# Relu rows of the later bias units one step ahead of their products, and the unpacking of the third weight matrix begun at the end of the second stage

## The chip, the cores and the metric

The kernel runs on one core of a Trainium2 chip. The metric is the device time of one execution in microseconds (us); the program is launched once and timed several times.

## What is computed

Attention with a learned position bias, followed by a gated product of matrices. For 4 batches, 8 heads, 576 positions and 64 channels a head:

```python
scores = (q @ k.T) / sqrt(64)
x = log1p(|i - j|) / log1p(max(i, 1))            # one number per pair of positions
bias = relu(x[..., None] * w1 + b1) @ w2         # 32 hidden units, one column of w2 per head
attn = softmax(scores + bias)
y = (attn @ v) as 2304 tokens x 512
out = ((y @ w_a) * (y @ w_b)) @ w_out            # 512 -> 1536 -> 512
```

All in 32-bit floats; the kernel splits operands into two 16-bit (or reduced 32-bit) parts and adds the products.

## The kernel before

**Score tiles.** The scores are made in 144 tiles of up to 128 rows by 576 columns (list `TILES`). The generator `attn_steps` has two steps for each tile. For tile n it loads the bias rows of tile n+2 from DRAM on SP's queue (`load_bias`, line 439), runs the *score step* (`soft1`: line 487 on VectorE adds scores and bias and takes the row minimum, line 492 on ScalarE takes the exponential), makes the score products of the next tile (`qk`, line 459, one PSUM buffer), transposes an earlier tile (`turn`, lines 535, 552, 554) and, once per unit of tiles, multiplies by v (`pv`, line 574). Three buffers hold loaded bias rows, so the load for a new tile waits for the score step three tiles before. `prep_k`, `prep_q` and `prep_v` (lines 385 to 423) prepare operands some tiles ahead.

**The gated products.** `moe_main` multiplies finished tokens by the first two matrices (`ab`, line 666, 24 steps), gates them (lines 674 and 676) and multiplies by the third (`o`, line 715, 12 steps). They fill TensorE between the score products. TensorE's order is the order in which the program is written; the function `merge` deals out the steps of several generators in proportion. The other engines' order is chosen by a scheduler, held by `late()`, which puts an instruction behind the newest score step, exponential and normalisation traced so far on its engine.

**Unpacking the weights.** The matrices arrive as 64-bit words. `w_unit` turns one chunk of 128 x 512 into 32-bit floats: line 256 on ScalarE scales the high words into a tile t, line 258 on VectorE shifts, line 259 merges the low words, line 262 merges the sign. `wo_split` then makes the two parts of a chunk of the third matrix on ScalarE (303) and GpSimd (304). `wo_steps` (its object is called `won`) does the 12 chunks of the third matrix, after a first step that only issues two loads. Raw words have three buffers, the tiles `wt` four.

**The bias table.** It is made on the chip, in 36 units of 16 rows (`bias_unit`). A unit takes the scaled logarithms u, forms four relu rows (line 134 on VectorE, line 138 on ScalarE; `nact` says how many are ScalarE's), multiplies them with w2 (line 144, four short products into PSUM), scales twice into `bo` (lines 161 and 164) and stores that to DRAM (line 166). Units 0 to 15 run at the start; the 20 *later units*, 16 to 35, run as a stream between the score tiles 46 to 61, while the batch that needs them is still to come. `stream[1]` lists at which tile a step of the stream is taken; each step does one unit whole. Their four row buffers h0 to h3 are single. A unit of up to 512 columns takes one of three PSUM buffers, a longer one two. The later units' u is loaded anew (line 117) when the unpacking of the third matrix is through, and scaled at line 119.

**Order around the change.** The second stage (main products of batch 0 beside score tiles 20 to 35) ends with `merge((main, 2 * FC - 19), (asteps, n1 - n1 * 4 // 5))`. The third opens with `merge((main, 2 * FC), (asteps, n2 * 2 // 3), (won, FC + 1))`: 24 product steps, 21 half tiles, and all of the third matrix. Then u is loaded and the stream begins.

Of the kernel before, what the change touches and what calls it, by code (L numbers as in the profile page):

```python
# [7 lines left out]
F32 = mybir.dt.float32  # L8
# [3 lines left out]
I32 = mybir.dt.int32  # L12
# [9 lines left out]
NU = S // 16  # L22
# [25 lines left out]
def attention_moe(ctx, tc, q0d, q1d, kd, vd, idn, wp, wa, wb, wo, lsw, lg, rl, out):  # L48
# [65 lines left out]

    def bias_windows(pool, tag, after=None):
        u = pool.tile([128, S], F32, tag=tag, name="u", bufs=1)
        nc.sync.dma_start(out=u, in_=lsw)
        with tc.issue_after(after.ins) if after else nullcontext():
            nc.vector.tensor_scalar(out=u, in0=u, scalar1=tab["w1"], scalar2=None, op0=ALU.mult)
        return u  # L120

# [23 lines left out]

    def bias_unit(bg, banks, u, un, nact, rows, bufs, queue):
        n = bias_span(un)
        hs = bias_relu(rows, u, un, nact)
        ob = bg.tile([128, BW], F32, tag="bo", name="bo", bufs=bufs)
# [16 lines left out]
        queue.dma_start(out=dst[:, :, :BW - 1], in_=ob[:, :BW - 1])  # L166
        yield

# [12 lines left out]
    @contextmanager  # L181
    def late():
        with ExitStack() as s:
            for x in (ttrs, exps, evs, pns):
                if x:
                    s.enter_context(tc.issue_after(x[-1].ins))
            yield
# [154 lines left out]
    def wo_steps(wt):  # L342
        raws = [w_load(wt, wo, f) for f in range(2)]
        yield
        for f in range(FC):
            with late():
                wf = w_unit(wt, raws[f])
                wo_split(f, wf)
            raws[f] = None
            if f + 2 < FC:  # L350
                raws.append(w_load(wt, wo, f + 2))
            yield
# [425 lines left out]
    with tc.tile_pool(name="bg", bufs=1, side="right") as bg, tc.tile_pool(name="eq", bufs=1, space=PSUM) as eq, \  # L778
# [6 lines left out]
        nc.vector.memset(tab["one"], 1.0)  # L785
        uls = bias_windows(att, "rk")

        def first_units(banks):
            for un in range(NU0):
                hs = cpool[0].tile([128, 4, S], F32, tag="pt", name="h", bufs=2)  # L790
                yield from bias_unit(
                    bh, lambda: banks(un), uls, un, int(un % 2 == 0 or un >= 8), lambda g: hs[:, g], 4, nc.gpsimd
                )

# [33 lines left out]
    run(wab)  # L828
    merge((main, 2 * FC - 19), (asteps, n1 - n1 * 4 // 5))
    ws.close()  # L830
    gpool[0] = ctx.enter_context(tc.tile_pool(name="gp", bufs=1, side="right", reuse_waits="tile"))

    def bias_stream(bg, u):
        for un in range(NU0, NU):
            yield from bias_unit(
                bg, lambda: mps.tile([128, 1, 2 * TOK], F32, tag="ab", name="psta", bufs=3), u, un, int(un % 4 != 3),
                lambda g: bg.tile([128, S], F32, tag=f"h{g}", name=f"h{g}", bufs=1), 2, nc.scalar,
            )

    nb = NU - NU0  # L840
    n2, n3 = steps(2)[1], 2 * ((ends[3] - ends[2]) * 2 // 3)
    main = moe_main(1, 0, mps)
    merge((main, 2 * FC), (asteps, n2 * 2 // 3), (won, FC + 1))
    run(won)
    wstack.close()
    with tc.tile_pool(name="bg2", bufs=1, reuse_waits="tile") as bg:
        uls = bias_windows(bg, "u", last[-12])
        stream[0] = bias_stream(bg, uls)
        first, nst = ends[1] + n2 // 3, ends[2] + n3 // 2 - ends[1] - n2 // 3
        stream[1] = [first + nst * i // nb for i in range(nb)]  # L850
        merge((main, GS + 1), (asteps, n2 - n2 * 2 // 3))
        xpool[0] = ctx.enter_context(tc.tile_pool(name="xp", bufs=1, side="right", reuse_waits="tile"))
        main = moe_main(2, 0, mps)
        merge((main, 2 * FC), (asteps, n3))
        run(stream[0])
# [61 lines left out]
```

## Time and profile before

| | |
|---|---|
| median of three timed runs | 846.47 us (843.23 to 848.3) |
| the profiled execution | 849.39 us, span of its instructions 847.6 us |
| TensorE busy | 775.6 us, 92% of the span |
| VectorE busy | 538.0 us, 63% |
| ScalarE busy | 511.6 us, 60% |
| GpSimd busy | 322.2 us, 38% |
| TensorE's mean granted clock | 0.953 of full speed |

Times in the trace count from the first instruction. PE is TensorE's products, PEld its weight loads, DVE VectorE, ACT ScalarE, POOL GpSimd, SP the engine that issues most loads. "busy" is the time inside instructions; an idle time in square brackets stands ahead of the instruction that ended it, with what released it behind the arrow. The granted clock is the share of full speed that TensorE got in a stretch. The third matrix is unpacked between about 210 and 278 us, the later bias units run from 280 to 382 us.

### The profile page before, as it was taken

Reading aid. Unit: us, or ns where it says so; the run is one execution under the profiler, and the core shown is the slowest. Engines: PE = TensorE matmul, PEld = TensorE weight load, DVE = VectorE, ACT = ScalarE, POOL = GpSimd, SP = SyncE. Lnnn points to the kernel's source line nnn. Section 1 sums busy time; section 2 is a strip of 40 time slices with the busy share of each in tenths; the row PEclk is TensorE's granted clock in tenths of the full one; section 3 lists DMA queues with packets and bytes.
Section 4 is the critical chain, followed back from the end, with each engine's and each line's share of the span. In section 5 each row is a group of like instructions: output and inputs, shape, how many; then the busy total and the mean of one; then the engine's idle time right before and its main releaser. Section 6 shows DMA issues by size and latency. Waiting matters only on the chain.

```text
span 847.6 us, 16500 instructions
## 1 busy us (share of the span) xinstructions
PE 775.6 (92%) x5960; PEld 621.3 (73%) x5960; DVE 538.0 (63%) x1243; ACT 511.6 (60%) x1102; POOL 322.2 (38%) x508
## 2 busy tenths in 40 slices
PE   4786779999878799979999999999999999999998
PEld 1244557668766566658888888988888898888886
DVE  4757778766899467874787777767776774110100
ACT  6667787656877467764676667656665665331310
POOL 1326667552765212321344334433442344220210
PEclk9957788999999799999999999999999999999999
DMA  8888675446773364543445444444434421100001
GB/s 284 282 270 225 204 204 157 138 120 199 225 224 99 98 181 143 152 134 89 140 126 142 137 141 121 113 137 143 122 117 129 129 74 52 58 1 26 2 11 39
DMA packets 51573, 114.16 MB, mean 135 GB/s; under 512 B 5156, under 2 KB 9508, under 8 KB 51492
## 3 DMA queue, kind: packets, MB, share of 16 engines
q1 hardware_dynamic: 44336, 97.34, 39.2%
q10 hardware_dynamic: 5876, 10.93, 4.4%
q0 software_dynamic: 1280, 4.84, 1.6%
q8 instruction: 47, 0.77, 0.4%
q14 instruction: 34, 0.28, 0.1%
HBM read 95.91 MB, written 17.18 MB: 133 GB/s over the span
## 4 chain that ended last, share of the span: by engine, by line
PE 68%; DVE 12%; DMA 9%; ACT 4%; issue 4%; POOL 1%; SPq 1%; ACTq 0%; DVEq 0%; POOLq 0%
PE ab L666 26%; PE o L715 18%; PE tp L535 8%; PE qk L459 8%; PE pv L574 5%; DMA rv<-vd 3%; DVE p L487 3%; PE psta L144 2%; DVE wt L262 2%; DMA bias<-bias_d 1%; DVE ks L386 1%; ACT p L492 1%; DMA rqf<-q0d 1%; DMA wraw<-wa 1%; DMA bias_d<-bo 1%
## 5 line engine op out<-in xcount | busy, mean ns | idle before, releaser
L666 PEld LDWEIGHTS <-w16t 128*128 128x128 f16 x2592 | 252.8, 99 | 46.8 <-issue 16.4
L666 PE MATMUL ab<-x,w16t 128*128 128x256 f16 x2304 | 273.2, 275 | 4.4 <-ACT bo L164 2.5
L487 DVE CUSTOM_DVE_ANT_0 p<-qk,bias 128x576 f32<-128x576 f32 x144 | 108.7, 755 | 92.6 <-PE tp L535 79.7
L522 POOL TENSOR_SCALAR p<-p,sm 128x576 f32<-128x576 f32 x144 | 127.9, 888 | 75.1 <-DVE sm L520 68.3
L552 ACT CAST pt<-tp 128x640 f16<-128x640 f32 x128 | 88.3, 690 | 95.3 <-PE tp L535 94.9
L492 ACT ACTIVATE p<-p,mn 128x576 f32<-128x576 f32 x144 | 111.7, 776 | 42.5 <-DVE mn L487 38.2
L535 PE MATMUL tp<-idn,p 128*128 128x128 f32 x720 | 110.5, 287 | 17.4 <-DVE pt L554 6.6
L715 PE MATMUL o<-wos,gh 128*128 128x512 f32 x384 | 124.4, 405 | 0.0
L691 POOL TENSOR_TENSOR gl<-g,gh 128x256 fp32r<-128x256 f32 x96 | 72.4, 754 | 131.7 <-ACT gh L690 130.5
L519 POOL TENSOR_SCALAR sm<-sm 128x1 f32<-128x1 f32 x144 | 30.2, 210 | 222.0 <-ACT p L492 218.4
L535 PEld LDWEIGHTS tp<-idn,p 128*128 128x128 f32 x720 | 86.7, 146 | 35.8 <-issue 19.9
L676 DVE SCALAR_TENSOR_TENSOR g<-ab,wv,asb 128x256 f32<-128x256 f32 x84 | 40.5, 482 | 81.3 <-ACT asb L674 80.7
L715 PEld LDWEIGHTS o<-wos,gh 128*128 128x128 f32 x384 | 69.1, 190 | 17.8 <-issue 5.4
L459 PE MATMUL qk<-ks,qs 128*128 128x288 f32 x384 | 72.4, 311 | 4.5 <-DVE mn L487 4.4
L715 PE MATMUL o<-wos,gl 128*128 128x512 f32 x192 | 75.7, 394 | 0.0
L144 PE MATMUL psta<-h,w2s 128*32 128x288 f32 (+17 forms) x352 | 50.8, 567 | 25.0 <-DVE h L134 16.4
L459 PEld LDWEIGHTS qk<-ks,qs 128*128 128x128 f32 x384 | 56.8, 190 | 9.7 <-DVE mn L487 6.5
L674 ACT ACTIVATE asb<-ab,wv 128x256 f32<-128x256 f32 x84 | 39.3, 467 | 37.7 <-PE ab L666 37.5
L690 ACT CAST gh<-g 128x256 fp32r<-128x256 f32 x96 | 38.8, 404 | 36.3 <-DVE g L676 36.2
L556 DVE TENSOR_TENSOR pt<-tp,pt 128x512 f16<-128x512 f32 x80 | 55.1, 689 | 8.0 <-ACT pt L552 7.9
L574 PE MATMUL pv<-pt,vs 128*64 128x320 f16 (+1 forms) x808 | 58.3, 299 | 0.0
L134 DVE TENSOR_SCALAR h<-u,lgs 128x576 f32<-128x576 f32 (+17 forms) x117 | 48.4, 471 | 12.6 <-PE psta L144 6.1
(98 smaller groups left out, 1017.6 us busy)
## 6 DMA issues: line engine op xcount, KB each, us to landing
bias<-bias_d SPq DMA_DIRECT2D x128, 288.0 KB
rv<-vd SPq DMA_DIRECT2D x40, 320.0 KB
rk<-kd SPq DMA_DIRECT2D x24, 288.0 KB
wraw<-wa SPq DMA_DIRECT2D x12, 512.0 KB
wraw<-wb SPq DMA_DIRECT2D x12, 512.0 KB
wraw<-wo SPq DMA_DIRECT2D x12, 512.0 KB
bias_d<-bo ACTq DMA_DIRECT2D x20, 295.5 KB
rq<-q1d SPq DMA_DIRECT2D x16, 320.0 KB
```

Of the source, the lines that this page charges most:

```text
L144: nc.tensor.matmul(dst[32 * g:32 * g + 32], tab["w2"], hs[g][:, c0:c1], start=True, stop=True)
L459: nc.tensor.matmul(ps[:, hf, :HB], a, b[:, hf * HB:hf * HB + HB], start=(x == 0), stop=(x == len(prods) - 1))
L487: ttr = nc.vector.tensor_tensor_reduce(out=p.rearrange("p (a n) -> p a n", a=2), in0=ps[:, :, :HB], in1=bt.rearrange("p (a n) -> p a n", a=2),
L492: exps.append(nc.scalar.activation(p, p, AF.Exp, bias=mn, scale=-1.0, accum_out=sm))
L522: nc.gpsimd.tensor_scalar(out=p, in0=p, scalar1=rc, scalar2=1.0, op0=ALU.mult, op1=ALU.mult)
L535: nc.tensor.transpose(tp[:, x, :], p[:, c0:c0 + 128], tab["idn"])
L552: nc.scalar.copy(dst[:, 0:5], src)
L556: nc.vector.tensor_tensor(out=dst[:, 5:9], in0=src[:, 0:4], in1=dst[:, 0:4], op=ALU.subtract)
L574: nc.tensor.matmul(ps[64 * j:64 * j + 64, :N], vs[:, part, vb, j, :], pt[:, pb, j * N:j * N + N], start=(x == 0), stop=(x == len(terms) - 1),)
L666: nc.tensor.matmul(ab[:, j], w16[nm, f][:, pw, kk, :], xs[px][:, kk, :], start=(x % (3 * KC) == 0), stop=(x % (3 * KC) == 3 * KC - 1),)
L691: nc.gpsimd.tensor_tensor(out=gl, in0=g, in1=gh.bitcast(F32), op=ALU.subtract)
L715: nc.tensor.matmul(o, g[:, sl], wos[f][:, p], start=(f == 0 and x == 0), stop=(f == FC - 1 and x == 2))
```

## The change

The relu rows leave `bias_unit`. `bias_stream` now scales u and makes the rows of unit 16 in a first step of its own; each later step makes the products of one unit and behind them the rows of the next, into the same single buffers. The stream so has 21 steps, dealt out over tiles 48 to 61 instead of 46 to 61. The scaling of u is queued by `late()` and no longer behind one of the last chunks. Four steps of `wo_steps` (its two first loads and three chunks) move into the last merge of the second stage, and the nine others share a merge with 22 product steps and 20 half tiles; the last two product steps go to the next merge. `w_unit` gets a tile of its own, wu, for the merged bits of the third matrix's chunks, so that line 262 reads the sign from t and not from the raw words. The first 16 units are only written differently.

```diff
+    def bias_scale(u):
+        with late():
             nc.vector.tensor_scalar(out=u, in0=u, scalar1=tab["w1"], scalar2=None, op0=ALU.mult)
...
-    def bias_unit(bg, banks, u, un, nact, rows, bufs, queue):
+    def bias_unit(bg, banks, un, hs, bufs, queue):
         n = bias_span(un)
-        hs = bias_relu(rows, u, un, nact)
...
-                wf = w_unit(wt, raws[f])
+                wf = w_unit(wt, raws[f], wt.tile([128, 512], I32, tag="wt", name="wu", bufs=4))
...
-    merge((main, 2 * FC - 19), (asteps, n1 - n1 * 4 // 5))
+    merge((main, 2 * FC - 19), (asteps, n1 - n1 * 4 // 5), (won, 4))
...
     def bias_stream(bg, u):
+        def rows(un):
+            return bias_relu(
+                lambda g: bg.tile([128, S], F32, tag=f"h{g}", name=f"h{g}", bufs=1), u, un, int(un % 4 != 3)
+            )
+
+        bias_scale(u)
+        hs = rows(NU0)
+        yield
         for un in range(NU0, NU):
-            yield from bias_unit(
-                bg, lambda: mps.tile([128, 1, 2 * TOK], F32, tag="ab", name="psta", bufs=3), u, un, int(un % 4 != 3),
-                lambda g: bg.tile([128, S], F32, tag=f"h{g}", name=f"h{g}", bufs=1), 2, nc.scalar,
-            )
-
-    nb = NU - NU0
+            bias_unit(bg, lambda: mps.tile([128, 1, 2 * TOK], F32, tag="ab", name="psta", bufs=3), un, hs, 2, nc.scalar)
+            if un + 1 < NU:
+                hs = rows(un + 1)
+            yield
+
+    nb = NU - NU0 + 1
...
-    merge((main, 2 * FC), (asteps, n2 * 2 // 3), (won, FC + 1))
+    merge((main, 22), (asteps, n2 * 5 // 8), (won, FC - 3))
...
-        uls = bias_windows(bg, "u", last[-12])
+        uls = bias_windows(bg, "u")
         stream[0] = bias_stream(bg, uls)
-        first, nst = ends[1] + n2 // 3, ends[2] + n3 // 2 - ends[1] - n2 // 3
+        first = ends[1] + n2 * 5 // 16 + 2
+        nst = ends[2] + n3 // 2 - first
         stream[1] = [first + nst * i // nb for i in range(nb)]
-        merge((main, GS + 1), (asteps, n2 - n2 * 2 // 3))
+        merge((main, 2 * FC - 22 + GS + 1), (asteps, n2 - n2 * 5 // 8))
```

VectorE behind the 35th score step (line 487; x, g, pt and sm belong to the tiles and products, wt, wu and wraw to the unpacking), before:

```order
L487 ISA p,mn<-qk,bias 128x576
L487 ISA mn 128x1
L676 SCALAR_TENSOR_TENSOR g<-ab,winv,asb 128x256
L554 TENSOR_TENSOR pt<-tp,pt 128x5x128
L520 RECIPROCAL sm<-sm 128x1
```

and now:

```order
L487 ISA p,mn<-qk,bias 128x576
L487 ISA mn 128x1
L258 TENSOR_SCALAR wu<-wt 128x512
L676 SCALAR_TENSOR_TENSOR g<-ab,winv,asb 128x256
L554 TENSOR_TENSOR pt<-tp,pt 128x5x128
L259 SCALAR_TENSOR_TENSOR wu<-wraw,wu 128x512
L520 RECIPROCAL sm<-sm 128x1
L258 TENSOR_SCALAR wu<-wt 128x512
L262 SCALAR_TENSOR_TENSOR wt<-wt,wu 128x512
```

The first chunk of the third matrix and the start of the second now stand here; before, the first chunk stood two score steps further on.

VectorE around the scaling of u for the later units, before, from the last preparation of v behind the 48th score step:

```order
L423 SCALAR_TENSOR_TENSOR vs<-rv,vs_3111,vs 128x640
L119 TENSOR_SCALAR u<-u,wps 128x576
L134 TENSOR_SCALAR h_3284<-u,lgs 128x320
L134 TENSOR_SCALAR h_3286<-u,lgs 128x320
L134 TENSOR_SCALAR h_3288<-u,lgs 128x320
L134 TENSOR_SCALAR h_3340<-u,lgs 128x304
```

and now, from the same preparation:

```order
L423 SCALAR_TENSOR_TENSOR vs<-rv,vs_3116,vs 128x640
L487 ISA p,mn<-qk,bias 128x576
L487 ISA mn 128x1
L122 TENSOR_SCALAR u<-u,wps 128x576
L554 TENSOR_TENSOR pt<-tp,pt 128x5x128
L136 TENSOR_SCALAR h_3335<-u,lgs 128x320
L136 TENSOR_SCALAR h_3337<-u,lgs 128x320
L136 TENSOR_SCALAR h_3339<-u,lgs 128x320
L520 RECIPROCAL sm<-sm 128x1
L136 TENSOR_SCALAR h_3352<-u,lgs 128x304
```

The scaling now stands behind the 49th score step, and a tile's line 554 stands between it and the first rows.

TensorE ahead of the first later unit's products, before, from the first output products behind a product with v:

```order
L715 MATMUL o<-wos_1261,gh 128x512 x2
L715 MATMUL o<-wos_1261,gl 128x512
L715 MATMUL o<-wos_1262,gh 128x512 x2
L715 MATMUL o<-wos_1262,gl 128x512
L144 MATMUL psta<-h_3284,w2s 32x320
```

and now, from the next tile's score products, which follow four chunks of output products:

```order
L459 MATMUL qk<-ks,qs 128x288 x4
L535 MATMUL tp<-idn,p 128x128 x5
L715 MATMUL o<-wos_1263,gh 128x512 x2
L715 MATMUL o<-wos_1263,gl 128x512
L715 MATMUL o<-wos_1264,gh 128x512 x2
L715 MATMUL o<-wos_1264,gl 128x512
L715 MATMUL o<-wos_1265,gh 128x512 x2
L715 MATMUL o<-wos_1265,gl 128x512
L715 MATMUL o<-wos_1266,gh 128x512 x2
L715 MATMUL o<-wos_1266,gl 128x512
L146 MATMUL psta<-h_3335,w2s 32x320
```

The unit's products have moved one tile back: eight chunks of output products stand ahead of them instead of two (three products a chunk), and one more score tile. Two units stand between two score products at four places before and at six now.

## Rows read from the trace of the kernel before

**Rows 1.** Busy us (instructions) of each engine by stretch; columns in the first line.

```profile
core 0: us, PE busy (x) PEld busy (x) DVE busy (x) ACT busy (x) POOL busy (x), PEclk, DMA share, GB/s
198.34:213.29 14.95, 12.18 (x118) 10.58 (x117) 9.23 (x21) 7.58 (x15) 2.81 (x6) 1.00 0.76 242
213.29:272.53 59.24, 50.52 (x431) 42.19 (x432) 55.70 (x111) 45.25 (x94) 37.99 (x45) 0.94 0.66 193
...
299.00:382.23 83.23, 76.17 (x675) 53.55 (x673) 60.75 (x131) 58.81 (x128) 23.65 (x41) 1.00 0.52 148
382.23:780.00 397.77, 396.58 (x3195) 345.96 (x3195) 249.62 (x580) 234.82 (x502) 140.45 (x249) 1.00 0.36 105
```

**Rows 2.** Timeline of ScalarE and VectorE: start us, us, instruction, [idle before].

```profile
210.52 0.68 ACT L256 ACTIVATE wt<-wraw 128x512 f32<-128x512 f32 x1 [3.45 <-DMA wraw<-wo]
...
211.23 0.43 DVE L258 TENSOR_SCALAR wt<-wt 128x512 int32<-128x512 int32 x1 [3.69 <-ACT wt L256]
...
272.53 0.74 DVE L487 CUSTOM_DVE_ANT_0 p<-qk,bias 128x576 f32<-128x576 f32 x1
...
273.81 0.81 DVE L554 TENSOR_TENSOR pt<-tp,pt 128x640 f16<-128x640 f32 x1
...
279.87 0.52 DVE L119 TENSOR_SCALAR u<-u,wps 128x576 f32<-128x576 f32 x1 [3.58 <-DMA u<-lsw]
280.42 0.98 DVE L134 TENSOR_SCALAR h<-u,lgs 128x320 f32<-128x320 f32 x3
```

**Rows 3.** The tile wt, 198 to 276 us: shortest/median/longest ns, starts.

```profile
L258 DVE TENSOR_SCALAR wt<-wt x12: 415/424/999, 211.2 to 268.2; 128x512 int32<-128x512 int32 x12
L259 DVE SCALAR_TENSOR_TENSOR wt<-wraw,wt x12: 667/688/1261, 211.7 to 270.8; 128x512 int32<-128x512 int32 x12
L262 DVE SCALAR_TENSOR_TENSOR wt<-wraw,wt x12: 669/758/1765, 212.7 to 273.2; 128x512 int32<-128x512 int32 x12
```

**Rows 4.** The loads of u and its scaling, first and last; size.

```profile
L117 SPq DMA_DIRECT2D u<-lsw x2: 382/400/418, 1.2 to 274.5; - x2
L119 DVE TENSOR_SCALAR u<-u,wps x2: 519/520/520, 4.3 to 279.9; 128x576 f32<-128x576 f32 x2
...
u<-lsw SPq DMA_DIRECT2D x2, 288.0 KB
```

**Rows 5.** TensorE: timeline, its busy time and clock, pieces of the chain.

```profile
214.10 0.82 PE L459 MATMUL qk<-ks,qs 128*128 128x288 f32 x4 [2.43 <-DVE mn L487]
...
216.03 3.83 PE L666 MATMUL ab<-x,w16t 128*128 128x256 f16 x24
...
280.87 1.87 PE L144 MATMUL psta<-h,w2s 128*32 128x320 f32 x8 [6.91 <-DVE h L134]
...
282.67:286.86 4.19, 4.19 (x18) 0.55 0.27 72
...
290.72 0.53 PE qk L459 x4
291.25 0.55 PE tp L535 x5
291.80 2.77 PE o L715 x12
```

**Rows 6.** TensorE's timeline in the bias stretch.

```profile
300.50 1.76 PE L144 MATMUL psta<-h,w2s 128*32 128x336 f32 x8 [0.56 <-DVE h L134]
...
308.20 0.80 PE L144 MATMUL psta<-h,w2s 128*32 128x352 f32 x8
...
324.52 1.97 PE L144 MATMUL psta<-h,w2s 128*32 128x416 f32 x8 [1.60 <-DVE h L134]
...
350.43 2.38 PE L144 MATMUL psta<-h,w2s 128*32 128x496 f32 x8 [0.64 <-ACT gh L690]
...
373.32 1.47 PE L666 MATMUL ab<-x,w16t 128*128 128x256 f16 x12 [2.50 <-ACT bo L164]
```

**Rows 7.** Idle ahead of the users of u, 270 to 390 us, by releaser.

```profile
  PE psta L144: 4.0, 10
```

More of the change, by code (lines that the diff above doesn't have):

```diff
@@ L113, in bias_tables, with bias_windows @@
         tab["w1"], tab["w2"], tab["b1l"], tab["rl"] = wps[:, 0:1], w2s, lgs, rls
-    def bias_windows(pool, tag, after=None):
+    def bias_windows(pool, tag):
         u = pool.tile([128, S], F32, tag=tag, name="u", bufs=1)
         nc.sync.dma_start(out=u, in_=lsw)
-        with tc.issue_after(after.ins) if after else nullcontext():
+        return u
+    def bias_scale(u):
+        with late():
             nc.vector.tensor_scalar(out=u, in0=u, scalar1=tab["w1"], scalar2=None, op0=ALU.mult)
-        return u
     def bias_span(un):
@@ L166, in bias_unit @@
         queue.dma_start(out=dst[:, :, :BW - 1], in_=ob[:, :BW - 1])
-        yield
     def bias_rows(h, i, n):
@@ L786, in attention_moe @@
         uls = bias_windows(att, "rk")
+        bias_scale(uls)
         def first_units(banks):
             for un in range(NU0):
-                hs = cpool[0].tile([128, 4, S], F32, tag="pt", name="h", bufs=2)
-                yield from bias_unit(
-                    bh, lambda: banks(un), uls, un, int(un % 2 == 0 or un >= 8), lambda g: hs[:, g], 4, nc.gpsimd
-                )
+                h4 = cpool[0].tile([128, 4, S], F32, tag="pt", name="h", bufs=2)
+                hs = bias_relu(lambda g: h4[:, g], uls, un, int(un % 2 == 0 or un >= 8))
+                bias_unit(bh, lambda: banks(un), un, hs, 4, nc.gpsimd)
+                yield
         def first_loads():
@@ L833, in bias_stream @@
     def bias_stream(bg, u):
-        for un in range(NU0, NU):
-            yield from bias_unit(
-                bg, lambda: mps.tile([128, 1, 2 * TOK], F32, tag="ab", name="psta", bufs=3), u, un, int(un % 4 != 3),
-                lambda g: bg.tile([128, S], F32, tag=f"h{g}", name=f"h{g}", bufs=1), 2, nc.scalar,
-            )
-    nb = NU - NU0
+        def rows(un):
[5 more added lines that the diff above has]
+        yield
+        for un in range(NU0, NU):
+            bias_unit(bg, lambda: mps.tile([128, 1, 2 * TOK], F32, tag="ab", name="psta", bufs=3), un, hs, 2, nc.scalar)
+            if un + 1 < NU:
+                hs = rows(un + 1)
+            yield
+    nb = NU - NU0 + 1
     n2, n3 = steps(2)[1], 2 * ((ends[3] - ends[2]) * 2 // 3)
     main = moe_main(1, 0, mps)
-    merge((main, 2 * FC), (asteps, n2 * 2 // 3), (won, FC + 1))
+    merge((main, 22), (asteps, n2 * 5 // 8), (won, FC - 3))
     run(won)
```

## The prediction

> **What bounds the kernel now.** I read the busy time by stretch first [rows 1]. From 382 us on TensorE is busy 396.58 of 397.77 us: nothing there can be shortened by moving other engines' work, and whatever is gained before it comes out at the end unchanged. Before that point the stretches differ. Between 213.29 and 272.53 us, which holds the unpacking of the third weight matrix (one row group of its three Vector steps in [rows 3]), VectorE is busy 55.70 of 59.24 us (94%) and TensorE 50.52: VectorE sets the pace. The 14.95 us ahead of it are slack on VectorE (9.23 busy). From 299 to 382 us TensorE is busy 76.17 of 83.23 again.
>
> Second, the Vector and Scalar rows [rows 2]. The first chunk of the third matrix reaches ScalarE only after 3.45 us of waiting for its load, and VectorE, which waits for ScalarE, stands still for 3.69 us. At 272.53 us begins a score step (line 487), the 48th in VectorE's order; I use it as the anchor. The scaling of u starts at 279.87, after 3.58 us of waiting for u's load.
>
> Third, TensorE's own waits [rows 5]. The largest of the whole middle of the kernel is 6.91 us, ended by a relu row, just before the first later bias unit's products at 280.87 us. Behind it TensorE's granted clock is 0.55 for 4.19 us, mostly the 1.2 GHz level instead of 2.4.
>
> **Part 1: the unpacking starts three score tiles earlier.** By the order, three chunks' Vector steps (lines 258, 259, 262) now stand behind the 35th, 36th and 37th score steps, and the remaining nine are spread one per tile instead of in twos. One chunk costs 0.42 + 0.69 + 0.76 = 1.9 us at the medians [rows 3]. Nothing is removed: line 262 reads the copy t instead of the strided raw words, at the same length of operand, so I cost that at nothing, and the new tile wu takes one of the same four buffers.
>
> What counts is VectorE from the 35th score step (198.34 us) to the 48th (272.53): 74.19 us, of which 9.23 + 55.70 = 64.9 are busy [rows 1]. The same instructions stand between those steps after the change, but for two that swap sides (one line 262 comes in, one gate product goes out; about even). Before, the first 15 us were 62% busy and the rest 94%. With work spread over all of it I take 94% throughout: 64.9 / 0.94 = 69.0 us, **5.2 us gained**. Ends: 0 (TensorE and the chain of score step, exponential and transpose set the pace as soon as VectorE does not) and 9.3 (VectorE never idle). I take the middle because the 94% is this same mixture of work and because the 3.7 us stall on the first load has a known cure: two of the loads now stand in SP's queue ahead of the previous tiles' bias loads, more than ten us before ScalarE asks for them. Their cover is that a bias load which they delay has two tiles until it is read. Should that cover fail, a score step waits for a load, some 3.5 us as the present one [rows 2].
>
> A chunk meets GpSimd less in its new place: GpSimd is busy 2.81 of 14.95 us there, against 37.99 of 59.24 later [rows 1], and the three steps range from 0.42, 0.67, 0.67 up to 1.00, 1.26 and 1.77 us [rows 3]. The Trainium skill (GPSIMD Engine Reference, Key points) says GpSimd shares its SBUF interfaces with VectorE and contends with two-input Vector instructions. By that rule the three moved chunks would take their shortest times, an estimated 2 us less in sum, so a gain near 7 us; the trace agrees in that lines 259 and 262, with two inputs, stretch far, but no row parts this from other causes, so I leave it out of the sum.
>
> **Part 2: the first unit's products stand one tile later, its rows with them.** On TensorE there now stand, ahead of these products, another score product, a transpose block and 18 more output products: 0.53 + 0.55 + 18/12 x 2.77 = 5.2 us [rows 5]. Where does the wait go? u's load is issued 1.97 us after the 48th score step starts, in either order behind the same 51 bias loads, and lands 5.37 us later [rows 2, 4]. Then come the scaling (0.52), now one subtraction for the score weights (0.81, line 554), and the first row (0.33 to 0.4): the products can start at 1.97 + 5.37 + 0.52 + 0.81 + 0.4 = 9.1 us behind the anchor. Before it was 280.87 - 272.53 = 8.3. So 0.8 us are lost and 5.2 us of other work are done meanwhile: **4.4 us gained**, and TensorE still waits about 6.9 + 0.8 - 5.2 = 2.5 us. What is late next is u's load again. Ends: the first load of u took only 3.1 us (4.3 - 1.2, [rows 4]); by that no wait is left and the gain is 6.9. At the other end u lands 2 us later, and it is 2.4.
>
> The Trainium skill (DMA: Bandwidth & Descriptors, Anatomy of one DMA) prices a DMA at about 2.0 us plus its bytes at 436 GB/s. By it u's 288 KB [rows 4] would need an estimated 2.7 us, the wait would be gone and the gain 6.9 us; the two loads in this trace, 3.1 and 5.37 us, are both longer.
>
> **Part 3: the clock behind that wait.** Behind the 6.91 us wait the work at 0.55 of the clock cost 4.19 x (1 - 0.55) = 1.9 us [rows 5]. A wait of 2.43 us at 214.10 was enough for the same: the 24 products behind it took 3.83 us, against two times 1.47 at full clock [rows 5, 6]. So with 2.5 us left I count half: **0.9 us gained** (ends 0 and 1.9).
>
> **Part 4: rows one step ahead, 20 units in 14 tiles instead of 16.** A unit alone in its tile has its rows ready now; only little was lost there before. Where two units stand in one tile, the second's rows still can't be made until the first's products have read the single row buffers, and its Scalar row stands behind two scalings of the first. Three such pairs in the trace cost wait plus overlength over a single block (0.80): 0.56 + 0.96, 1.60 + 1.17, 0.64 + 1.58, so 1.5 to 2.8, mean 2.2 us [rows 6]. Before there are four pairs, after six. At the mean that is 4.3 us more; against it, the 2.50 us wait at 373.32 may go. Two of the six have their second unit's rows all on VectorE and should be cheaper. I take **1.0 us lost**, ends 2.5 gained and 4.3 lost.
>
> **Sum.** 5.2 + 4.4 + 0.9 - 1.0 = 9.5 us. The profiled execution took 849.39 us for a span of 847.6; by it 839.9. It lies 2.9 us over the median of the three timed runs, 846.47, which is what I predict against: 846.5 - 9.5 = **837.0 us**. A change under 0.5% (4.2 us) can hardly be told from none.
>
> **Rivals.** (a) VectorE was not the limit, the chain of one tile to the next was: part 1 gives nothing, the rest 4.3 us, 842.2 us. For it: TensorE and VectorE are only 5 us apart in [rows 1]; against it: waits that end on Vector unpacking rows. (b) u lands in time and the clock holds: 5.2 + 6.9 + 1.9 - 1.0 = 13.0, 833.5 us. The first load of u speaks for it, the second against. By the Trainium skill's price of a DMA, above, this is where it would come out. (c) The pairs cost the dearest row each, 6 x 2.8 against 4 x 2.2, 8 us, and part 1 half: 2.6 + 4.4 + 0.9 - 8.0, no change, 846.6 us. (d) Slower: the rows of the next unit are queued on VectorE right behind the present unit's products and ahead of the next score step, because the row buffers are single. VectorE then stands in a wait for TensorE, with the score step behind it and TensorE's next transpose behind that. If each of 19 such waits holds the next score step by one block of products, 0.9 us, that is 17 us lost and 7.5 slower in all, 854 us. It decides from 0.5 us each (9.5 / 19). Today such waits are 4.0 us in 10 [rows 7]; against it stands that by the order the products come ahead of the score product that the next score step needs, so the wait should end in time.
>
> **Chances.** Forecast 0.55, (a) 0.17, (b) 0.12, (c) 0.10, (d) 0.06. Faster by over 0.5%: the forecast, (b) and two thirds of (a), 0.78; within 0.5%: (c) and the rest of (a), 0.16; slower 0.06. The range reaches from (b) with a further 3 us of part 1, 830.5, to just past (a), 843.5; it leaves out (c), (d) and some tails.
>
> **What would show it.** Part 1: the 48th score step starts near 267 us, no Vector wait for the first chunk, and no products wait for it. Part 2: TensorE's wait before the first later unit falls from 6.9 to 2 to 3 us, ended by u's load. Part 3: granted clock above 0.55 behind it. Part 4: six pairs with 1 to 2 us each, singles with none; TensorE's idle time in the bias stretch about as before. Wrong would be: a 48th score step still at 272 us (then (a)), Vector rows waiting for products by more than 0.5 us each (then (d)), or a span that changes behind the last bias unit.

## The result, and the profile after

The changed kernel takes 836.11 us (median of five runs, 835.59 to 839.09), the kernel before 844.68 us in the same comparison. The ratio is 0.9893, with an interval from 0.9866 to 0.9920: 9.0 us faster (6.8 to 11.3); the two medians differ by 8.6. The prediction was 837.0 us and 9.5 us faster.

The two profiled spans, 847.6 and 834.3 us, differ by 13.3 us, and that has to be split before anything is read from it. The 35th score step starts at 198.34 us before and at 193.60 after, although TensorE, VectorE and GpSimd have done the same instructions in the same order by then (ScalarE has one line 256 more, and two loads of raw words stand ahead). Twelve further traces, of kernels that are the same or nearly so up to there, have it between 193.18 and 196.23; among them e2, which unpacks as before, is at 195.88 and e1, which unpacks early, at 196.10. So I count 4.74 us of the 13.3 as the scatter of two executions. The programs are equal again from the 64th score step on, and from there to the last (the 144th) the traces take 329.00 and 329.05 us. What the change did lies between: 188.05 us before, 179.47 after, 8.58 us less.

I cut that stretch at the 48th and the 50th score step, as the prediction's first two parts do. The rows give the stretch, its length, then busy us (instructions) of PE, PEld, DVE, ACT and POOL, the granted clock, the DMA share and GB/s. Before:

```profile
198.34:272.53 74.19, 62.69 (x549) 52.76 (x549) 64.94 (x131) 52.83 (x109) 40.80 (x51) 0.95 0.68 202
272.53:291.84 19.31, 12.40 (x59) 8.65 (x59) 8.81 (x24) 7.71 (x17) 5.95 (x7) 0.73 0.32 83
291.84:386.39 94.55, 87.49 (x736) 62.30 (x736) 67.30 (x144) 65.17 (x139) 25.31 (x44) 1.00 0.51 146
```

After, with the long rest that answers to the last row of [rows 1]:

```profile
193.60:261.12 67.52, 58.92 (x542) 50.54 (x541) 65.72 (x132) 51.37 (x109) 43.41 (x51) 0.97 0.69 201
261.12:275.48 14.36, 12.41 (x61) 9.66 (x58) 8.23 (x20) 6.47 (x14) 5.12 (x7) 0.88 0.38 107
275.48:373.07 97.59, 89.57 (x744) 62.86 (x744) 68.53 (x148) 66.80 (x143) 25.54 (x44) 1.00 0.50 142
...
380.00:770.00 390.00, 388.82 (x3147) 339.41 (x3146) 245.82 (x573) 231.04 (x495) 139.49 (x247) 1.00 0.36 107
```

Length minus busy PE is TensorE's idle time: 11.50, 6.91 and 7.06 us before, 8.60, 1.95 and 8.02 after. So 2.9 us were gained in the unpacking, 5.0 ahead of the first later unit, and 1.0 lost in the bias stretch, 6.9 together. The remaining 1.7 us are a smaller busy time (162.58 to 160.90 us) for the same 1342 instructions.

The waits of TensorE in the trace of after, but for four of 0.65 to 0.76 us during the unpacking (start, length; in brackets the idle time ahead and what ended it):

```profile
215.55 0.74 PE L535 MATMUL tp<-idn,p 128*128 128x128 f32 x5 [2.25 <-DVE pt L554]
...
239.05 0.74 PE L535 MATMUL tp<-idn,p 128*128 128x128 f32 x5 [1.77 <-DVE pt L554]
...
270.01 1.23 PE L146 MATMUL psta<-h,w2s 128*32 128x320 f32 x8 [1.95 <-DVE h L136]
...
284.52 1.61 PE L146 MATMUL psta<-h,w2s 128*32 128x320 f32 x8 [0.94 <-DVE h L136]
...
298.14 1.82 PE L146 MATMUL psta<-h,w2s 128*32 128x368 f32 x8 [0.58 <-DVE h L136]
...
310.76 1.97 PE L146 MATMUL psta<-h,w2s 128*32 128x416 f32 x8 [1.61 <-DVE h L136]
...
325.90 2.11 PE L146 MATMUL psta<-h,w2s 128*32 128x464 f32 x8 [0.63 <-DVE h L136]
...
339.48 2.62 PE L146 MATMUL psta<-h,w2s 128*32 128x512 f32 x8 [0.65 <-ACT gh L690]
...
356.13 1.88 PE L146 MATMUL psta<-h,w2s 128*32 128x288 f32 x16 [1.19 <-DVE h L136]
...
365.35 1.47 PE L666 MATMUL ab<-x,w16t 128*128 128x256 f16 x12 [2.42 <-ACT bo L165]
```

The 6.91 us of [rows 5] have become 1.95, the pairs of [rows 6] are still there, two more of them, and the 2.50 us wait of a gate product for a scaling, last in [rows 6], is still there as well, at 2.42. Around u's load:

```profile
261.12 0.74 DVE L487 CUSTOM_DVE_ANT_0 p<-qk,bias 128x576 f32<-128x576 f32 x1
...
263.07 0.38 SPq L117 DMA_DIRECT2D u<-lsw  x1
...
268.31 0.52 DVE L122 TENSOR_SCALAR u<-u,wps 128x576 f32<-128x576 f32 x1 [2.20 <-DMA u<-lsw]
```

The load is issued 1.95 us behind the start of the 48th score step and its user starts 5.24 us later, nearly as before [rows 2, 4].

### The profile page after: what moved, and what is told of

The parts are those of the page before. It is cut to its first block, busy times and chain, and to the rows that moved or that the text cites. A ratio compares the mean times of both kernels' runs of the same rounds, so it can differ in the third digit from the quotient of the medians.

```text
span 834.3 us, 16512 instructions
## 1 busy us (share of the span) xinstructions
PE 767.6 (92%) x5960; PEld 616.4 (74%) x5960; DVE 542.2 (65%) x1243; ACT 510.6 (61%) x1102; POOL 325.4 (39%) x508
## 4 chain that ended last, share of the span: by engine, by line
PE 70%; DVE 13%; DMA 7%; issue 5%; ACT 4%; POOL 1%; SPq 1%; ACTq 0%; DVEq 0%; POOLq 0%
PE ab L666 27%; PE o L715 18%; PE qk L459 8%; PE tp L535 8%; PE pv L574 6%; PE psta L146 2%; DVE p L487 2%; DMA bias<-bias_d 2%; DMA rqf<-q0d 2%; DVE ks L386 1%; DVE wt L262 1%; DMA wraw<-wa 1%; DVE wu L259 1%; ACT p L492 1%; DVE pt L554 1%
## 5 line engine op out<-in xcount | busy, mean ns | idle before, releaser
L535 PE MATMUL tp<-idn,p 128*128 128x128 f32 x720 | 107.4, 281 | 17.9 <-DVE pt L554 7.1
L519 POOL TENSOR_SCALAR sm<-sm 128x1 f32<-128x1 f32 x144 | 32.4, 225 | 210.0 <-ACT p L492 206.4
L535 PEld LDWEIGHTS tp<-idn,p 128*128 128x128 f32 x720 | 84.7, 143 | 35.0 <-issue 22.7
```

The source lines that it names most:

```text
L535: nc.tensor.transpose(tp[:, x, :], p[:, c0:c0 + 128], tab["idn"])
```

## Experiments

All ratios are to the kernel before on the same chip in the same comparison; its median lay between 843.69 and 846.23 us. A gain in us is taken from the ratio, with its 95% interval in brackets. A difference of two ratios under about 0.003 can't be told from none.

### The two halves apart

e1: the kernel before, with the unpacking begun early and the tile wu, and nothing else.

```diff
+                wf = w_unit(wt, raws[f], wt.tile([128, 512], I32, tag="wt", name="wu", bufs=4))
...
-    merge((main, 2 * FC - 19), (asteps, n1 - n1 * 4 // 5))
+    merge((main, 2 * FC - 19), (asteps, n1 - n1 * 4 // 5), (won, 4))
...
-    merge((main, 2 * FC), (asteps, n2 * 2 // 3), (won, FC + 1))
+    merge((main, 2 * FC), (asteps, n2 * 2 // 3), (won, FC - 3))
```

> The kernel before with one half of the change alone: four steps of the third matrix's unpacking go into the last merge of the second stage, with the tile wu; the stream of later units is as before. Theory A (the unpacking costs the middle of the kernel by TensorE's idle time, and the trace of after, with 2.9 us less of it between the 35th and the 48th score step and some 1.2 us less in the length of equal products, shows its whole worth): 3 to 5 us faster than before, so near 840.5 us, with 6 to 8 us of wait left ahead of the first later unit. Theory B (VectorE's span between these two score steps is the worth, 6.7 us in the trace of after): near 838 us. Rival (a) of the prediction (VectorE was not the limit): no gain, 844.7 us.

Measured: 840.87 us, ratio 0.9944 (0.9924 to 0.9963), 4.7 us faster (3.1 to 6.4). This is Theory A's time. Rival (a) of the prediction, that this part gives nothing, falls with the interval. Whether the stretch was held by VectorE's work as a whole or by its stall on the first load [rows 2] is not parted by this run. The wait ahead of the first unit's products is still there, at 5.88 us a little under the 6 to 8 expected:

```profile
273.26 1.87 PE L144 MATMUL psta<-h,w2s 128*32 128x320 f32 x8 [5.88 <-DVE h L134]
```

e2: the changed kernel with the unpacking put back, so that only the stream differs from before.

```diff
...
+        bias_scale(u)
+        hs = rows(NU0)
+        yield
         for un in range(NU0, NU):
-            yield from bias_unit(
...
+            bias_unit(bg, lambda: mps.tile([128, 1, 2 * TOK], F32, tag="ab", name="psta", bufs=3), un, hs, 2, nc.scalar)
+            if un + 1 < NU:
+                hs = rows(un + 1)
+            yield
...
-    nb = NU - NU0
+    nb = NU - NU0 + 1
...
```

> The kernel before with the other half alone: u is scaled and the rows of unit 16 are made in a step of their own, the rows of each unit one step ahead, 21 steps over tiles 46 to 61; the unpacking is as before. Theory A: the first unit's products wait for u about 2 us in place of 6.9, the clock behind gives back about 1 us, and pairs cost about as before or 1 us more: 4 to 6 us faster than before, near 839.5 us. With the unpacking's half the two gains add up to the whole, 8.6 us. Theory C (the two halves need each other: the wait that one removes comes back at the next place that is late): under 2 us faster, and the two gains sum to less than 6 us.

Measured: 842.56 us, ratio 0.9959 (0.9944 to 0.9974), 3.5 us faster (2.2 to 4.7), a little under Theory A. When the list of the stream is set, 21 half tiles of the stage are through, the first half of tile 46 with them, so two entries for tile 46 fall out, here as in the kernel before. There the first unit so comes in tile 47; here the scaling does, and the first unit's products stand in tile 48, one tile later. The wait has gone from 6.91 to 2.95 us:

```profile
277.31 1.87 PE L146 MATMUL psta<-h,w2s 128*32 128x320 f32 x8 [2.95 <-DVE h L136]
```

4.7 and 3.5 us make 8.2, against 9.0 for the whole. Within their intervals the halves add up, and Theory C falls.

### Are rows one step ahead worth anything?

e3: the changed kernel with each unit's rows in the step of its own products.

```diff
-        hs = rows(NU0)
         yield
         for un in range(NU0, NU):
+            hs = rows(un)
             bias_unit(bg, lambda: mps.tile([128, 1, 2 * TOK], F32, tag="ab", name="psta", bufs=3), un, hs, 2, nc.scalar)
-            if un + 1 < NU:
-                hs = rows(un + 1)
             yield
```

> The changed kernel, but each later unit's rows are made in the step of its own products again, not one step ahead; the early unpacking, the late scaling of u and the tiles of the products stay. Theory A (single units lost little by late rows, and pairs can't have theirs ahead with single row buffers anyway): within 2 us of after, 835 to 838 us. Theory D (the rows queued ahead are what carries the later units): waits of 0.5 to 1 us before each single unit come back, 4 to 8 us, 840 to 844 us. Rival (d) of the prediction (rows queued ahead hold VectorE and cost time): 1 to 3 us faster than after.

Measured: 837.66 us, ratio 0.9893 (0.9872 to 0.9913), the changed kernel's to the last digit. The cause is plain once the two built programs are laid side by side: with buffer numbers left out, all five engines have the same instructions in the same order, but for one preparation step on VectorE that stands two places earlier. The relu rows are not among what `late()` holds; the scheduler puts them where their buffers come free, and where they stand in the code hardly matters. Of the change's title, the first half builds nothing new. That leaves, for what e2 gained, the step ahead of the first unit, which moves all products of the stream back by up to a tile; e13, below, moves that place. Rival (d) can't be tested by a run that builds the same program; against it stands that the rows it feared wait in VectorE's queue before the change as well [rows 7].

### What the pairs cost

e7: the changed kernel, but the second of two units that fall on one tile is taken in the second half of the tile, behind main products.

```diff
-            for _ in range(stream[1].count(n)):
+            if n in stream[1]:
                 next(stream[0], None)
...
             yield
+            for _ in range(stream[1].count(n) - 1):
+                next(stream[0], None)
             if n + 1 < N0:
```

> The changed kernel with one rule altered: where two steps of the stream fall on one tile, the second is taken in the second half of the tile, so that main products stand between the two units. Theory A (the idle time of the bias stretch, 8.0 us in the trace of after, belongs to the pairs): most of the pairs' waits go, 3 to 6 us faster than after, 830 to 833 us. Rival E (the waits belong to ScalarE, which scales each unit twice, and only move): within 1.5 us of after, 835 to 837.5 us.

Measured: 824.11 us, ratio 0.9738 (0.9717 to 0.9760): 12 us faster than the changed kernel by the medians, 13 by the ratios, twice the most that I expected. The cause is Theory A's, and rival E falls. Its three stretches:

```profile
193.18:260.77 67.59, 58.88 (x542) 50.41 (x541) 65.80 (x131) 51.40 (x109) 43.42 (x51) 0.97 0.67 200
260.77:272.98 12.21, 10.85 (x61) 8.44 (x58) 8.23 (x20) 6.38 (x14) 5.12 (x7) 1.00 0.38 101
272.98:359.26 86.28, 86.00 (x744) 61.65 (x744) 68.59 (x148) 65.90 (x144) 25.82 (x44) 1.00 0.58 162
```

The bias stretch falls from 97.59 to 86.28 us. 7.7 of these 11.3 us were idle time, and 3.6 us were hidden in busy time, 89.57 against 86.00 for the same 744 instructions. The rule also moved the first unit: tile 48 holds two steps, the scaling and the first unit, so that unit's products now stand in the second half of the tile, behind six more output products. The wait for u is 1.36 us in place of 1.95, the clock behind it stays full, and the middle row is 12.21 us long against 14.36. The 2.1 us there are no more than the same program scatters by in that row (12.61 us in e3, 14.82 in c1); the 11.3 us are the pairs' and the gate product's (its 2.42 us wait has gone too). One pair of the changed kernel shows both kinds of loss:

```profile
308.27 0.88 PE L146 MATMUL psta<-h,w2s 128*32 128x400 f32 x8
308.38 0.75 DVE L487 CUSTOM_DVE_ANT_0 p<-qk,bias 128x576 f32<-128x576 f32 x1
...
309.06 0.48 DVE L676 SCALAR_TENSOR_TENSOR g<-ab,wv,asb 128x256 f32<-128x256 f32 x1
...
309.45 0.81 DVE L554 TENSOR_TENSOR pt<-tp,pt 128x640 f16<-128x640 f32 x1
...
310.19 1.60 DVE L136 TENSOR_SCALAR h<-u,lgs 128x416 f32<-128x416 f32 x3
...
310.62 0.58 ACT L165 ACTIVATE bo<-psta,rls 128x399 f32<-128x399 f32 x1
...
311.09 0.64 ACT L140 ACTIVATE h<-u,lgs 128x416 f32<-128x416 f32 x1
```

The first unit's products end at 309.15 us. VectorE, in a score step by then, still does a gate product and line 554 and reaches the rows of the second unit at 310.19; TensorE stands for 1.61 us (the row at 310.76, above). Then its block takes 1.97 us in place of about 0.9, because its rows come one after another: VectorE's third is done at 311.79 and ScalarE's, behind two scalings, at 311.73. In e7 the rows of this unit stand behind the same steps on both engines, and 24 main products lie between the units:

```profile
303.14 0.88 PE L146 MATMUL psta<-h,w2s 128*32 128x400 f32 x8
...
303.95 2.79 PE L668 MATMUL ab<-x,w16t 128*128 128x256 f16 x24
...
306.67 0.91 PE L146 MATMUL psta<-h,w2s 128*32 128x416 f32 x8
```

A second set of row buffers, the other way to part the two units, was not tried.

e9: e7 with the rows in the step of their own products, the edit of e3.

> The kernel of e7 with each unit's rows made in the step of its own products, as in e3. Theory A (rows ahead are worth something only where the row buffers are free for them, which the split pairs now give): 2 to 6 us slower than e7, 826 to 830 us. Theory H (rows one step ahead are worth nothing here either, the products stand behind enough main products): within 1.5 us of e7, 822.5 to 825.5 us.

Measured: 823.66 us, ratio 0.9759 (0.9737 to 0.9781). Theory H has the time, for the same reason as in e3: the order on all engines is e7's, without a single exception. The pair e7 and e9 also shows what two comparisons of one program differ by: 0.0021 in the ratio.

e8: the rule of e7 on the kernel before.

> The kernel before with the one rule of e7: a second later unit in a tile is taken in the tile's second half. Theory A (a pair costs its wait and its overlength, in the trace of before 1.6, 2.7, 2.0 and 2.9 us for four pairs, and the 2.5 us wait of a gate product behind a scaling is of the same kind): 9 to 12 us faster than before, 833 to 836 us, less than the 12.0 us it gave on the changed kernel with its six pairs or about that. Theory B (the gain of e7 needs the rows one step ahead, which only the changed kernel has): under 5 us.

Measured: 838.28 us, ratio 0.9933 (0.9910 to 0.9957), 5.7 us faster (3.6 to 7.6): less than Theory A; B's "under 5 us" lies inside the interval. The bias stretch gives 8.1 us, 86.44 against 94.55, with one unit less in it (728 products against 736); but the wait ahead of the first unit is longer than before:

```profile
289.56:376.00 86.44, 83.32 (x728) 60.84 (x728) 65.78 (x140) 63.44 (x137) 24.83 (x44) 1.00 0.54 156
```

```profile
263.72 0.40 PE L717 MATMUL o<-wos,gl 128*128 128x512 f32 x1
273.01 1.78 PE L144 MATMUL psta<-h,w2s 128*32 128x320 f32 x8 [8.90 <-DVE h L134]
274.72 1.33 PE L459 MATMUL qk<-ks,qs 128*128 128x288 f32 x4
...
277.05 2.85 PE L574 MATMUL pv<-pt,vs 128*64 128x256 f16 x30
```

The rule itself did that. Of the two entries for tile 46 that fell out before, it takes one in the second half of that tile, so on TensorE, whose order is the program's, the first unit's products stand ahead of a score product, a block of transposes and a product with v that stood ahead of them before. So e8 has the rule's gain on the pairs and, against it, a first unit half a tile earlier; by how much the pairs alone would gain on the kernel before, no run shows. On VectorE the scaling stands behind the 47th score step instead of the 48th. From the 35th to the 64th score step this trace takes 181.31 us, 6.7 less than before.

### The wait for u, and the clock behind it

e4: no load of u, a fill of a constant in place of the scaling.

```diff
-        bias_scale(u)
+        with late():
+            nc.vector.memset(u, 0.5)
...
-        uls = bias_windows(bg, "u")
+        uls = bg.tile([128, S], F32, tag="u", name="u", bufs=1)
```

> The changed kernel without the later units' load of u: a fill of constant 0.5 on VectorE stands where the scaling stood (the later bias rows are computed from that constant). It takes the wait for u away and nothing else. Theory A (after still pays that wait, 1.95 us, and behind it the lower clock, granted 0.66 from 270.01 to 275.00 us, some 1.6 us): 3 to 4 us faster than after, 832 to 833 us. Theory B (only the wait): 834 us. Theory C (the first rows or the score step are late next): within 1 us of after.

Measured: 835.70 us, ratio 0.9900 (0.9879 to 0.9920), no faster than the changed kernel (0.9893). Only C has the time, and C's reason isn't there: nothing is late next. The stretches:

```profile
194.04:264.49 70.45, 61.53 (x542) 52.20 (x541) 65.15 (x131) 52.00 (x109) 42.42 (x51) 0.93 0.70 195
264.49:275.13 10.64, 10.64 (x61) 8.35 (x58) 8.03 (x20) 6.37 (x14) 5.12 (x7) 1.00 0.37 96
275.13:374.31 99.18, 91.16 (x744) 64.13 (x744) 68.51 (x147) 66.81 (x142) 25.54 (x44) 0.98 0.50 142
```

In the middle row the gain is there in full: no idle time, full clock, 3.7 us less than after's 14.36. It is given back ahead and behind, in rows whose busy time is 2.6 and 1.6 us longer at the same work: the clock was lower there, 0.93 against 0.97 and 0.98 against 1.00.

c1: the changed kernel once more, for a second trace.

> The changed kernel once more, unaltered, for a second trace. Theory A (a wait of TensorE fixes the lower clock that follows it): the granted clock falls at the same two places as in the first trace of after, some 22 and 76 us behind the 35th score step, and the 35th to the 64th score step take 179.5 us again. Theory K (whether the clock falls behind a wait of some 2 us differs from execution to execution of one kernel, as the traces of the other runs suggest): the waits are the same within 0.3 us, but one of the falls is missing or stands behind another wait, and the stretch differs by 1 to 3 us.

Measured: 837.70 us, ratio 0.9891 (0.9861 to 0.9921). Five us behind each of the four largest waits, in the first trace of after:

```profile
215.55:220.50 4.95, 4.95 (x44) 3.87 (x45) 4.95 (x9) 3.57 (x8) 3.43 (x4) 0.66 0.74 212
239.05:244.00 4.95, 4.95 (x57) 3.96 (x58) 4.95 (x10) 4.11 (x10) 4.09 (x5) 1.00 0.77 222
270.01:275.00 4.99, 4.99 (x21) 3.64 (x22) 1.95 (x6) 1.34 (x3) 0.74 (x1) 0.66 0.24 64
365.35:370.30 4.95, 4.95 (x39) 4.46 (x39) 2.68 (x8) 2.67 (x6) 0.92 (x2) 1.00 0.68 196
```

and in the second:

```profile
216.97:221.90 4.93, 4.93 (x44) 3.76 (x45) 4.93 (x9) 3.56 (x8) 3.43 (x4) 0.65 0.73 219
240.45:245.40 4.95, 4.95 (x57) 3.95 (x58) 4.95 (x10) 4.25 (x9) 4.08 (x5) 1.00 0.79 216
271.86:276.85 4.99, 4.99 (x21) 3.50 (x22) 1.94 (x6) 1.34 (x3) 0.74 (x1) 0.66 0.24 63
367.18:372.10 4.92, 4.92 (x30) 4.32 (x30) 2.07 (x6) 1.84 (x4) 0.73 (x1) 0.65 0.65 193
```

The waits are the same (2.25 and 2.28, 1.77 and 1.76, 2.42 and 2.42 us; only the one for u differs, 1.95 and 2.41). Behind the last one the clock stays full once and falls to 0.65 once, where 30 products are done in five us and not 39; this stretch is 1.6 us longer for it. That is Theory K. In the trace of e5 (below), with nearly the same waits (2.25, 1.76, 1.64 and 2.42 us), the clock falls behind the first two and neither of the others. So the price of a single wait can't be read from one trace, and e4's missing gain is partly this: its trace has falls behind the second wait (2.47 us there) and the fourth, which after's first trace lacks. That the timed runs, several of each, don't show e4 faster either is not explained by one trace. By the intervals up to some 2 us of gain may be hidden; 3 to 4 are not. What e4 gains stays open.

### Where the first products stand

e13 and e11: e7 with the stream started one tile earlier (shown) and one later (+ 3).

```diff
-        first = ends[1] + n2 * 5 // 16 + 2
+        first = ends[1] + n2 * 5 // 16 + 1
```

> The kernel of e7 with the stream started one tile earlier (tile 47), so that the first later unit's products stand about six chunks of output products, a score product and a transpose block further ahead on TensorE, some 5.2 us of work; u's load stays where it is. Theory A (the products' place against u's arrival is what the second half of the change gains): the wait ahead of them rises from 1.4 to 6 to 7 us with a lower clock behind it, 4 to 6 us slower than e7, 828 to 830 us. Theory H (the place does not matter, since the waiting time is made up elsewhere): within 1.5 us of e7, 822.5 to 825.5 us.

Measured: 833.24 us, ratio 0.9858 (0.9837 to 0.9880), 9 to 10 us slower than e7, twice Theory A.

```profile
268.59 1.78 PE L146 MATMUL psta<-h,w2s 128*32 128x320 f32 x8 [4.73 <-DVE h L136]
...
359.41 2.55 PE L668 MATMUL ab<-x,w16t 128*128 128x256 f16 x12 [2.42 <-ACT bo L165]
```

The wait for u rises from 1.36 to 4.73 us; the wait of a gate product for a scaling, which e7 lost, is back; and behind both the clock is low, so that TensorE is busy 158.7 us from the 35th to the 64th score step, against 155.7 in e7. Of the 9.4 us between the two traces there, 6.6 lie between the 48th and the 50th score step, where one unit more stands, and 2.9 behind it, where the gate product's wait is. Theory H falls. Theory A has the direction, but a longer wait for u (6 to 7 us) and not the second wait.

> The kernel of e7 with the stream started one tile later (tile 49): 20 units in 13 tiles, u has landed when the first products come. Theory A: the last 1.4 us of wait go and nothing is late next, 1 to 2 us faster than e7, 822 to 823 us. Rival I (more units to a tile make rows or scalings late): 1 to 4 us slower, 825 to 828 us.

Measured: 824.73 us, ratio 0.9765 (0.9743 to 0.9786), at best e7's time. The wait for u is gone, and 0.55 us for a row of ScalarE's has come instead:

```profile
275.87 0.72 PE L146 MATMUL psta<-h,w2s 128*32 128x320 f32 x2 [0.55 <-ACT h L140]
```

Over these three places the time is flat once the products stand about where u arrives or behind, and rises ahead of that, in part by a wait that is not u's.

### Two smaller edits

e5: the changed kernel without wu.

```diff
-                wf = w_unit(wt, raws[f], wt.tile([128, 512], I32, tag="wt", name="wu", bufs=4))
+                wf = w_unit(wt, raws[f])
```

> The changed kernel without the tile wu: line 262 takes the sign from the raw words again, and a chunk needs one of the four wt buffers instead of two. Theory A (the prediction's price of nothing): within 1.5 us of after, 834.5 to 837.5 us. Rival F (raw words are held until line 262, and their next load is later, on a VectorE that is busy 97% of that stretch): 2 to 4 us slower, 838 to 840 us. Rival G (two wt buffers a chunk make ScalarE's line 256 wait): 1 to 3 us faster.

Measured: 836.82 us, ratio 0.9911 (0.9889 to 0.9933). Theory A holds: wu costs and gains nothing that can be measured.

e10: e7 with six unpacking steps in the second stage.

```diff
-    merge((main, 2 * FC - 19), (asteps, n1 - n1 * 4 // 5), (won, 4))
+    merge((main, 2 * FC - 19), (asteps, n1 - n1 * 4 // 5), (won, 6))
...
-    merge((main, 22), (asteps, n2 * 5 // 8), (won, FC - 3))
+    merge((main, 22), (asteps, n2 * 5 // 8), (won, FC - 5))
```

> The kernel of e7 with six instead of four steps of the third matrix's unpacking in the last merge of the second stage, seven left for the third. Theory A (VectorE sets the pace between the 35th and the 48th score step, and any of its work moved ahead of that is gained): up to two chunks of 1.9 us, 1 to 4 us faster than e7, 820 to 823 us. Theory J (the raw words' three buffers, or the scheduler, hold the chunks back, or VectorE is no longer what is late): within 1 us of e7.

Measured: 825.04 us, ratio 0.9770 (0.9745 to 0.9795), no gain. Theory J: in this build the first chunk stands behind the 35th score step as in e7, and only some later chunks a step or two earlier, so nothing was moved out of the stretch, which takes 67.58 us again. Which of Theory J's causes holds the chunks there, and whether VectorE would give more, stays open.

## Why the prediction was right, point by point

The total was right (9.5 us predicted, 9.0 measured). By TensorE's trace, in which the terms must add up to the time, parts 1, 3 and 4 each hold a step that was wrong, and their errors nearly cancel.

**Part 1, 5.2 us predicted.** The quantity that I forecast came as said: from the 35th to the 48th score step 67.52 us, forecast 69.0, with VectorE busy 65.72 of it (97%). The stall of VectorE on the first chunk [rows 2] is gone; ahead of line 258 the idle time was 4.2 us and is 0.2:

```profile
L258 DVE TENSOR_SCALAR wt<-wt 128x512 int32<-128x512 int32 x12 | 6.8, 581 | 4.2 <-ACT wt L256 4.1
```

```profile
L258 DVE TENSOR_SCALAR wu<-wt 128x512 int32<-128x512 int32 x12 | 6.3, 527 | 0.2
```

But that quantity is VectorE's, and the end is set by TensorE. In the trace of before, TensorE did seven output products ahead of the 48th score step (the stretch, its length, then the busy time of PE and PEld on the tile o alone):

```profile
198.34:272.53 74.19, 1.86 (x7) 1.28 (x8) 0.00 (x0) 0.95 0.68 202
```

After, none of them: they have moved behind it. Of the 6.7 us by which the interval shrank, 1.9 are this moved work and no gain. TensorE's idle time fell by 2.9, and the last 1.9 are shorter busy time of the work that stayed, at a granted clock of 0.97 against 0.95. **The failed step: I measured part 1 between two VectorE instructions and part 2 from the second of them by TensorE's order. Six of the 18 output products that part 2 counts as more work during the wait had stood ahead of that instruction before, so that their going shortened part 1's interval as well: the same products were credited in both.** The 5.2 us came near what was gained (2.9 of idle time and 1.9 of clock here, 4.7 in e1) because VectorE was busier, 97%, than the 94% I took. The 1.9 are not sure to be the change's: with TensorE's order the same, e5 has 0.95 and 60.57 us busy against 58.92.

**Part 2, 4.4 us predicted.** Idle time ahead of the first unit fell by 5.0 us, from 6.91 to 1.95 (2.5 foretold), ended by u's load as said. u was issued 1.95 us behind the anchor and used 5.24 us later; the forecast had 1.97 and 5.37. The Trainium skill's price of a DMA (DMA: Bandwidth & Descriptors, Anatomy of one DMA) is a fit for DMAs that GpSimd issues, and u's load is issued by SP; taken over to it, an estimated 2.7 us, there would be no wait. The trace disagrees, with 5.24 us and a wait of 1.95.

**Part 3, 0.9 us predicted.** The step as I put it is wrong. Half the low clock should have gone with the shorter wait; behind u's wait the clock is 0.66 for 4.99 us in both traces of after (4.99 x 0.34 = 1.7 us, against 1.9 behind the 6.91), and behind 1.36 us in e7 it isn't low at all. From the 35th to the 64th score step TensorE's busy time fell by 1.7 us, though the blocks of the pairs hold 1.6 us more (part 4), so the clock gave some 3.3 us in this one trace: the 1.9 of part 1 and 1.4 elsewhere. c1 gives 1.6 of them back. What the clock gives belongs to no one place.

**Part 4, 1.0 us lost predicted.** TensorE's idle time in the bias stretch rose by 1.0 us, and the block lengths behind pairs, which [rows 6] show as overlength, hold more: apart from the first block, the later units' products are busy 24.4 - 1.9 = 22.5 us before and 25.3 - 1.2 = 24.1 after. Together 2.6 us lost, where I had 1.0. The mean price of 2.2 us a pair was good: waits and overlengths of the six pairs are 1.8, 1.6, 2.7, 1.8, 2.2 and 1.9 us, mean 2.0. The failed step is the credit against it: I let the 2.50 us wait at 373.32 go, and it stayed (2.42). And the heading of the part has nothing behind it: rows made one step earlier in the code stand where they stood on VectorE (e3).

So by the trace of TensorE the terms are 4.8 (1.9 of it clock), 5.0, 1.4 and -2.6, together 8.6 us, where I had 5.2, 4.4, 0.9 and -1.0. That the sum agreed to half a microsecond is luck, with a clock term that moves by 1.6 us from one execution to the next. The halves e1 and e2, 4.7 and 3.5 us, would have been forecast at 5.2 and 4.3; both lie inside the intervals, so the times alone don't show which term was off.

**Rivals.** (a), nothing gained by part 1, is excluded by e1. (b) did not come: the wait was 1.95 us and the clock behind it 0.66. (c) took part 1 at half, 2.6 us, near the 2.9 of idle time but under e1's 4.7, and took 8 us for the pairs, which cost 2.6. (d): VectorE's rows did wait for products, in the bias stretch 3.8 us in 10 waits, against 2.8 us in 8 in the same list and stretch of before (4.0 in 10 over the longer stretch of [rows 7]):

```profile
DVE h L136 <- PE psta L146: 3.8, 10, 0.9
```

That is 0.38 us each, hardly more than the 0.35 before and under the 0.5 from which (d) decides.

## What to carry to other kernels

Cut a stretch at one engine's instructions only to time that engine; for a sum over parts, use idle time of the engine that sets the end, and see on which side of the cut its work lies. Where a scheduler sets an engine's order, look at the built order before pricing a line that was moved in the code: here the rows one step ahead built the same program. And where two dependent blocks stand back to back on the bounding engine, put independent work between them: on the changed kernel that small rule (e7) was worth more, some 12 us, than the whole change. On the kernel before it gave 5.7, since it moved the first unit as well (e8): look at everything such a rule moves.

## What the runs showed of the hardware that I had not expected

Behind one and the same TensorE wait of about 2 us, the granted clock falls to the lower level in one execution and stays full in the next (2.42 us: 0.65 and 1.00 over five us). Where it falls, rows of two us reach 0.50, the 1.2 GHz level, and one fall cost about 1.6 us. Ahead of the 35th score step the slowest trace, before at 198.3 us, has a mean clock of 0.85 and 156.85 us busy on TensorE, after (193.6 us) 0.89 and 150.43 for the same 1022 products; all fourteen traces lie between 0.84 and 0.89, the three at 0.89 being the three shortest. So the clock is the likely cause of that scatter; no run separates it.

The 288 KB of u took 4.62 (e1) to 6.25 us (e10) from issue to the start of their user, wherever that user waited for the load, and always behind the same 51 bias loads in SP's queue; the first load of u had taken 3.1 [rows 4].

Beginning three chunks earlier did not shorten the unpacking in sum: lines 258, 259 and 262 took 6.8 + 10.4 + 10.9 = 28.1 us before and 6.3 + 11.2 + 11.1 = 28.6 after. Nor is GpSimd nearly idle in their new place, as the prediction read from [rows 1]: a chunk brings its own GpSimd step (line 304) with it. In the first 14.95 us behind the 35th score step GpSimd was busy 2.81 us before, and after (columns as in [rows 1]) 9.73:

```profile
193.60:208.55 14.95, 12.34 (x117) 10.57 (x117) 14.88 (x33) 10.80 (x23) 9.73 (x10) 1.00 0.85 250
```

The nine Vector steps of the three moved chunks still took 5.7 us, near their shortest times (5.3) and under the 7.0 of three mean chunks; the other nine chunks took more than before, 2.5 us each against 2.3. By the Trainium skill (GPSIMD Engine Reference, Key points), GpSimd contends with two-input Vector instructions for the SBUF interfaces they share; the 2 us that I estimated from it are not in the sum, and no run parts this from other causes.
